# A gated unit and a long convolution on one core: the inverse transform's turn partly moved from DRAM to VectorE, and its neighbours made longer

## The chip, the cores and the metric

The kernel runs on one core of a Trainium2 chip. The metric is the device time of one execution in microseconds (us). Of the kernel before three executions were timed: the median is 236.9 us, the lowest 236.68, the highest 237.43. A change of about 0.3% (0.7 us) is what such a measurement can still tell from no change.

The core has five engines with instruction streams of their own: TensorE (PE; its weight loads are PEld in the profile), VectorE (DVE), ScalarE (ACT), GpSimd (POOL) and SyncE (SP). SP here does nothing but issue DMAs, and ACT issues a few. Each engine works its instructions off in program order; between engines there are only semaphores.

## The reference

The input `x` has 2048 rows of 640. It is layer-normalized to `xn`, and three things are added up: `x` itself, a convolution branch A and a gated branch B.

```python
x = A_q
xn = _layernorm(x, axis=-1)
return x + _A_ref(xn, A_k, A_v, A_shift_k, A_ssm_k, A_ssm_D) + _B_ref(xn, B_w_gate, B_w_up, B_w_down)
# B:  h = sigmoid(xn @ w_gate) * (xn @ w_up);  h @ w_down           (640 -> 1728 -> 640)
# A:  k_shift = four shifted copies of k times four taps, summed;  kv = k_shift * v
#     y = causal convolution of kv with ssm_k along the 2048 rows (by a real FFT of length 4096)
#     y = y + kv * ssm_D;   result xn * y
```

## The kernel before

Row `16*p + b` of the sequence lies on partition `p`, block `b` (16 blocks). Branch B runs in four passes `t` of 512 rows: for each of 13 slices of the hidden size a gate product and an up product (`product`, L293, five 512-column matmuls each), the sigmoid on ACT (`gate_ev`, L302), the product of the two on DVE (`up_ev`, L308), then a last half slice (`both_*`) and the down products (`down_mm` L334, `pair_mm` L341, `rest_mm` L351), whose sums DVE adds to `x` (L345, L356).

Branch A runs in five chunks `c` of 128 channels, woven between the products. A chunk goes through these steps:

- `kv_op` (chain `k`): the four shifted products and three sums on DVE (L384, L388, L390), and the product with `v` (L393). Each operation covers half of the blocks (128x1024), so there are 16 per chunk. `h_turn` (L370) transposes the filter by 32x32 blocks on DVE.
- `st1_mm`, `st1_ev`, `wr1`: the first transform stage on PE, copies out of PSUM into `t1` by ACT or DVE (L256, L259), and a write to DRAM (`d1`).
- `rd2`, `st2_mm`, `st2_ev`, `prod`: the turned data is read back, second stage in 32x32 matmuls (L443), copies into `xz`, and the complex product with the filter on DVE (L456 shuffle, L458 product).
- `inv1_mm`, `inv1_ev`: first inverse stage (PE L472), copies into `ao` by ACT or DVE.
- `wr2`, `rdb`: the turn of the inverse. `ao` is written to DRAM (`d2`, L488 in one piece or L492 in two) and read back with another assignment of partitions into `bi` (L502), two reads per chunk.
- `inv2_mm`, `inv2_q`, `inv2_x`: second inverse stage (PE L511, eight 128-column matmuls per group `m`, four groups per chunk), the product with `xn` on DVE (L516, 128x512) and the addition to `x` on DVE (L521, 128x512).

`store` (L359) writes finished pieces of `x` out, all on SP's queue but the very last, which ACT issues.

The order is written out by hand: every step is appended to a chain named by a letter, and the string `ORDER` names, letter by letter, which chain emits its next step. `F`, `I` and `J` mean that a copy out of PSUM (`B`, `A`, `C`) goes to DVE instead of ACT. `TURNS` reorders two chains, the loads `m` and the stores `o`. So each engine's program order, SP's queue of DMAs among them, is this string's order. PSUM has two pools: `psC` (two buffers, branch A's stages) and `psG` (four buffers, the products of branch B and of `inv2_mm`).

Of the kernel before, what the change touches and what calls it, by code (L numbers as in the profile page):

```python
# [37 lines left out]
def _tables():  # L38
# [11 lines left out]
    tb = s1.transpose(3, 2, 1, 0) / 2048.0  # L50
# [15 lines left out]
def kernel(  # L66
# [57 lines left out]
    kxs = [res.tile([P, NB + 3, P], BF16, name="kx%d" % i) for i in range(2)]  # L124
# [233 lines left out]
    def store(b0, b1, lo, hi):  # L358
        (nc.scalar if b1 == NB and hi == DM else sync).dma_start(outr[:, b0:b1, lo:hi], x[:, b0:b1, lo:hi])  # L359
# [12 lines left out]
    def kv_op(c, n):  # L372

        d = cin[c]
        half, n = divmod(n, 8)
        lo, hi = 8 * half, 8 * half + 8
        sc = d["sc"]
        kx = kxs[c % 2]
        def sb(m):
            return sc[:, m:m + 1, :].to_broadcast((P, 8, P))  # L380

        if n == 0:
            d["acc"] = cv.tile([P, 8, P], BF16, name="acc")
            nc.vector.tensor_tensor(d["acc"][:, :, :], kx[:, lo + 3:hi + 3, :], sb(0), ALU.mult)  # L384
        elif n in (1, 3, 5):
            m = (n + 1) // 2
            d["tmp"] = cv.tile([P, 8, P], BF16, name="tmp")
            nc.vector.tensor_tensor(d["tmp"][:, :, :], kx[:, lo + 3 - m:hi + 3 - m, :], sb(m), ALU.mult)  # L388
        elif n in (2, 4, 6):
            nc.vector.tensor_tensor(d["acc"][:, :, :], d["acc"][:, :, :], d["tmp"][:, :, :], ALU.add)  # L390
        else:
            kv = d["kvh"][:, 0, lo:hi, :]
            nc.vector.tensor_tensor(kv, d["acc"][:, :, :], kv, ALU.mult)  # L393
# [19 lines left out]
    def st1_ev(c, n, copy=act_copy):  # L413
        d = chunks[c]
        if n % 2 == 0:
            d[n // 2] = cv.tile([P, 8, 2, P], BF16, name="t1", bufs=2)
        o = 4 * (n % 2)
        copy(out=d[n // 2][:, o:o + 4, :, :].rearrange("p b s c -> p s b c"), in_=pss[n][:, :, :, :])

    def wr1(c, k):  # L420
        h, part = divmod(k, 2)
        d = chunks[c]
        sync.dma_start(d["d1"][:, h, 8 * part:8 * part + 8, :], d[k].rearrange("p b s c -> p b (s c)"))

    groups = {}
    xz = cv.tile([P, 3, 3, 8, P], BF16, name="xz")

    def rd2(s):

        c, s4 = divmod(s, 4)  # L430
# [5 lines left out]
    def st2_mm(s):  # L436

        d = groups[s]
        d["ps"] = ps = [psC.tile([P, 2, 2, 2, P], F32, name="ps2", tag="c") for _ in range(2)]
        for e in range(2):  # L440
            for g in range(4):
                for q in range(NQ):
                    nc.tensor.matmul(ps[q // 2][quad(g), q % 2, e, :, :], lhsT=FW[quad(q), 8 * (s % 4) + 2 * g + e, :],  # L443
# [17 lines left out]
    def inv1_mm(y):  # L461
# [3 lines left out]
        if y2 == 0:  # L465
            d["d2"] = dr.tile([32, P, P], BF16, name="d2", bufs=NC)
# [9 lines left out]
    def inv1_ev(y, n, copy=act_copy):  # L476
        d = chunks[y // 2]
        if n == 0:
            d["ao", y] = kxs[1][:, 0:NB, :] if y >= 7 and y % 2 else cv.tile([P, 16, P], BF16, name="ao")[:, :, :]
        dst = d["ao", y].rearrange("p (s g e) c -> p g s (e c)", s=2, g=4)  # L480
# [3 lines left out]
    def wr2(y):  # L484
        c, y2 = divmod(y, 2)
        d = chunks[c]
        if 2 * y % 3 < 2:
            sync.dma_start(d["d2"][16 * y2:16 * y2 + 16].rearrange("r p c -> p r c"), d["ao", y])  # L488
# [5 lines left out]
    def rdb(c, n):  # L494

        d = chunks[c]
        if c >= 3 and n == 1:
            bi = kxs[0][:, 0:NB, :].rearrange("p (h b) c -> p h b c", h=2)
        else:
            bi = cv.tile([P, 2, 8, P], BF16, name="bi")[:, :, :, :]  # L500
        src = d["d2"].rearrange("r (q h b) c -> (r q) h (b c)", q=NQ, h=2)
        sync.dma_start(bi.rearrange("p h b c -> p h (b c)"), src[:, :, 1024 * n:1024 * n + 1024])  # L502
        d["bi", n] = bi

    def inv2_mm(c, m):

        bi = chunks[c]["bi", m // 2]
        chunks[c]["pb", m] = ps = psG.tile([P, 4, P], F32, name="psb", tag="g")
        for i in range(4):
            for h in range(2):  # L510
                nc.tensor.matmul(ps[:, i, :], lhsT=TB[:, h, 4 * m + i, :], rhs=bi[:, h, 4 * (m % 2) + i, :],  # L511
                                 start=(h == 0), stop=(h == 1))

    def inv2_q(c, m):
        chunks[c]["yx", m] = yx = cv.tile([P, 4, P], BF16, name="yx")
        nc.vector.tensor_tensor(yx[:, :, :], chunks[c]["pb", m][:, :, :], xn[:, 4 * m:4 * m + 4, c * P:(c + 1) * P],  # L516
                                ALU.mult)

    def inv2_x(c, m):
        xs = x[:, 4 * m:4 * m + 4, c * P:(c + 1) * P]  # L520
        nc.vector.tensor_tensor(xs, xs, chunks[c]["yx", m][:, :, :], ALU.add)  # L521
# [120 lines left out]
    for c in range(NC):  # L642
# [15 lines left out]
        for y in (2 * c, 2 * c + 1):  # L658
# [3 lines left out]
            step("W", wr2, y)  # L662
        for n in range(2):
            step("R", rdb, c, n)
        for m in range(4):
            step("d", inv2_mm, c, m)
            step("q", inv2_q, c, m)
            step("q", inv2_x, c, m)
        for n in range(16):
# [28 lines left out]
    mmmmgggmssggmuLuLmsggsZgmugmgmLsuuggsmgggsmkLkgkkkumsmgkusmmgkPgmullmlgulHmgsusgmHmuggDgggmkksuskkaA  # L698
    kkkanggkkHaTAAegKuHeawmtkegkkekLgugaAuAgkkaADLgguaawAukmgsgAkggTuLksakkkkkggsguuwLPAkmkaAsthgggsKaaH
    HwVAAugukggaamwsskKKrukkkwkkAAklgggauADkksVggTbwlguBgakssglBkkkAuspprgbBgguBkasnkaKKwIggthTuaAkaugAI  # L700
    suggawspHuLLklkVkkAkkawApggakaLsgkkAKkgeemgAceLPuuggrgHuuCCbBrekkwgVFgkgppDlkkaAauKAggwhsulbgtgBBrwk
# [43 lines left out]
```

## Time and profile before

| | |
|---|---|
| median of the runs | 236.9 us |
| the profiled execution's own time | 238.36 us |
| its span, first to last instruction | 236.5 us |
| PE busy | 227.2 us, 96% |
| DVE busy | 202.1 us, 85% |
| ACT busy | 134.7 us, 57% |
| DMA, queue of SP | 55.42 MB, 89.3% of 16 engines' span |

The span is what the profile explains; some 1.9 us of the profiled execution's time lie around it. Durations in the profile are those of single instructions and overlap by some hundredths of a microsecond where one follows another at once. A matmul's duration is longer than the step from one matmul to the next, because matmuls are pipelined.

### The profile page before, as it was taken

How to read it: one execution, taken by the hardware profiler on the slowest of the kernel's cores; microseconds unless marked ns; L12 is line 12 of the kernel's file. 1: busy time of each engine (PE TensorE's matmuls, PEld its weight loads, DVE VectorE, ACT ScalarE, POOL GpSimd, SP SyncE). 2: the span in 40 equal slices, each digit the busy share in tenths (PEclk: the TensorE clock that was granted, in tenths of full speed). 3: DMA queues.
4: the chain of work that ended last, by engine and by line, in shares of the span. 5: the costliest groups of instructions: out<-in, count | busy, mean ns of one | idle time of the engine just before them, and what ended most of it. 6: DMA issues, size and time to landing. Idle time of an engine off the chain costs nothing.

```text
span 236.5 us, 5598 instructions
## 1 busy us (share of the span) xinstructions
PE 227.2 (96%) x2281; PEld 112.0 (47%) x2281; DVE 202.1 (85%) x321; ACT 134.7 (57%) x197; POOL 12.1 (5%) x27
## 2 busy tenths in 40 slices
PE   8999999979999999999999999999999999999990
PEld 2854444436444444447444445445654444445480
DVE  5542983899898989999998999999999999999591
ACT  2458521368886686993976566566365684651000
POOL 4210020000040000020000000000000000000000
PEclk9999999999999999999999999999999999999998
DMA  6999997997999997799999996899999885684775
GB/s 181 305 264 267 256 306 180 236 230 209 231 274 276 301 238 208 140 226 306 282 245 255 298 333 138 219 242 257 247 288 269 224 237 176 173 247 110 222 242 160
DMA packets 98223, 56.13 MB, mean 237 GB/s; under 512 B 56342, under 2 KB 92438, under 8 KB 98070
## 3 DMA queue, kind: packets, MB, share of 16 engines
q1 hardware_dynamic: 97622, 55.42, 89.3%
q8 instruction: 18, 0.29, 0.5%
q10 hardware_dynamic: 576, 0.36, 0.5%
q14 instruction: 7, 0.06, 0.1%
HBM read 35.45 MB, written 18.35 MB: 228 GB/s over the span
## 4 chain that ended last, share of the span: by engine, by line
PE 63%; DVE 15%; SPq 9%; DMA 8%; issue 3%; DVEq 0%
PE pg L293 16%; PE pu L293 16%; PE pd L334 13%; PE pr L351 4%; DMA kx<-in_A_k_dram 4%; PE ps L409 4%; PE ps L411 4%; DMA w<-in_B_w_up_dram 3%; DVE yx L516 3%; PE ps L443 2%; PE psa L472 2%; SPq L185 2%; DVE x L521 2%; SPq L188 2%; DVE xz L458 2%
## 5 line engine op out<-in xcount | busy, mean ns | idle before, releaser
L293 PEld LDWEIGHTS <-w 128*128 128x128 bf16 x500 | 47.0, 98 | 58.1 <-issue 4.8
L293 PE MATMUL pu<-xnT,w 128*128 128x512 bf16 x250 | 62.3, 380 | 0.0
L293 PE MATMUL pg<-xnT,w 128*128 128x512 bf16 x250 | 62.2, 379 | 0.0
L334 PE MATMUL pd<-wd,hT 128*128 128x512 bf16 x208 | 48.4, 379 | 0.3 <-DMA wd<-in_B_w_down_dram 0.2
L308 DVE TENSOR_TENSOR hT<-sig,pu 128x512 bf16<-128x512 bf16 x52 | 35.0, 682 | 12.5 <-PE pu L293 6.8
L302 ACT ACTIVATE sig<-pg 128x512 bf16<-128x512 f32 x52 | 30.9, 601 | 23.8 <-PE pg L293 20.3
L256 ACT CAST xz<-ps 128x1024 bf16<-128x1024 f32 x33 | 32.4, 1017 | 16.8 <-PE ps L443 16.8
L256 ACT CAST t<-ps 128x1024 bf16<-128x1024 f32 x33 | 32.5, 1011 | 16.6 <-PE ps L411 14.7
L334 PEld LDWEIGHTS <-hT 128*128 128x128 bf16 x208 | 19.7, 98 | 24.9 <-issue 2.7
L458 DVE TENSOR_TENSOR xz<-xz 128x2048 bf16<-128x2048 bf16 x20 | 24.4, 1220 | 0.3
L390 DVE TENSOR_TENSOR acc<-acc,tmp 128x1024 bf16<-128x1024 bf16 x30 | 20.7, 689 | 0.6
L388 DVE TENSOR_TENSOR tmp<-kx,sc 128x1024 bf16<-128x1024 bf16 x30 | 20.7, 689 | 0.5
L409 PE MATMUL ps<-kvh,S1t 128*128 128x512 bf16 x40 | 15.2, 379 | 1.2 <-DVE kvh L393 1.2
L411 PE MATMUL ps<-kvh,S1t 128*128 128x512 bf16 x40 | 15.5, 387 | 0.0
L456 DVE STREAM_SHUFFLE xz<-xz 128x512 f32<-128x512 f32 x20 | 14.5, 725 | 0.0
L516 DVE TENSOR_TENSOR yx<-psb,xn 128x512 bf16<-128x512 f32 x20 | 13.7, 685 | 0.7
L351 PE MATMUL pr<-wd,hT 128*128 128x128 bf16 x224 | 14.2, 219 | 0.0
L351 PEld LDWEIGHTS <-hT 128*128 128x128 bf16 x224 | 13.1, 98 | 2.0 <-issue 0.6
L256 ACT CAST ao<-psa 128x1024 bf16<-128x1024 f32 x11 | 10.8, 1013 | 4.0 <-PE psa L472 2.6
L345 DVE TENSOR_TENSOR x<-pd,x 128x512 bf16<-128x512 f32 x16 | 10.6, 683 | 2.9 <-PE pd L341 2.3
L511 PEld LDWEIGHTS <-TBt 128*128 128x128 bf16 x160 | 10.1, 98 | 3.6 <-issue 0.7
L370 DVE STREAM_TRANSPOSE kvh<-hn 128x512 f32<-128x512 f32 x10 | 10.9, 1096 | 0.0
(62 smaller groups left out, 189.3 us busy)
## 6 DMA issues: line engine op xcount, KB each, us to landing
d<-t SPq DMA_DIRECT2D x20, 512.0 KB, 5.2
t<-d SPq DMA_DIRECT2D x20, 512.0 KB, 5.3
bi<-d SPq DMA_DIRECT2D x8, 512.0 KB, 8.6
d<-ao SPq DMA_DIRECT2D x6, 512.0 KB, 5.3
kx<-in_A_k_dram SPq DMA_DIRECT2D x10, 256.0 KB, 5.2
kvh<-in_A_v_dram SPq DMA_DIRECT2D x10, 256.0 KB, 5.4
hn<-in_A_ssm_k_dram SPq DMA_DIRECT2D x20, 128.0 KB, 5.8
x<-in_A_q_dram SPq DMA_DIRECT2D x3, 640.0 KB, 5.4
```

What stands on the lines that cost most here:

```text
L256: nc.scalar.copy(out=out, in_=in_)
L293: nc.tensor.matmul(pg[:, :], lhsT=w[:, c, u * UP + fc * P:u * UP + (fc + 1) * P], rhs=xnT[:, :, c, :], start=(c == 0), stop=(c == NC - 1))
L302: nc.scalar.activation(sig[fc][:, :], pgs[0, fc][:, :], ACT.Sigmoid)
L308: nc.vector.tensor_tensor(hT[:, fc, :], sig[fc][:, :], pgs[1, fc][:, :], ALU.mult)
L334: nc.tensor.matmul(pds[bb][:, :], lhsT=hT[:, fc, bb * P:(bb + 1) * P], rhs=wd[:, fc, 0:4 * P], start=(fc == 0), stop=(bb > 1 and fc == NFC ...
L351: nc.tensor.matmul(pds[t, b0][:, bb, :], lhsT=hT[:, fc, bb * P:(bb + 1) * P], rhs=wd[:, fc, 4 * P:DM], start=(fc == 0), stop=(fc == NFC - 1))
L388: nc.vector.tensor_tensor(d["tmp"][:, :, :], kx[:, lo + 3 - m:hi + 3 - m, :], sb(m), ALU.mult)
L390: nc.vector.tensor_tensor(d["acc"][:, :, :], d["acc"][:, :, :], d["tmp"][:, :, :], ALU.add)
L409: nc.tensor.matmul(ps[:, 0, :, :], lhsT=S1[:, h, :], rhs=cin[c]["kvh"][:, 0, 4 * n4:4 * n4 + 4, :], start=True, stop=True)
L411: nc.tensor.matmul(ps[:, 1, :, :], lhsT=S1[:, h, :], rhs=hp[:, 2 * n4:2 * n4 + 2, :, :], start=True, stop=True)
L458: nc.vector.tensor_tensor(z[:, 1:3, :, :], z[:, 0:1, :, :].to_broadcast((P, 2, 8, P)), z[:, 1:3, :, :], ALU.mult)
L516: nc.vector.tensor_tensor(yx[:, :, :], chunks[c]["pb", m][:, :, :], xn[:, 4 * m:4 * m + 4, c * P:(c + 1) * P], ALU.mult)
```

## The change

- **The inverse turn.** For chunks 0 and 1 it still goes through DRAM, now written in one piece per half chunk and read back by four DMAs, each into 32 partitions (`rdb(c, q)`), in place into `ao`. For chunks 2, 3 and 4 there is no DMA: `inv_turn` transposes `ao` in place on DVE, four operations of 128x512 four-byte elements per chunk. `ao` is now one tile for a whole chunk, its own for chunks 0 to 2, the memory of `kx` for chunk 3 and that of `t1` for chunk 4. The table `TB` is permuted to suit, and `rows` swaps two groups of some chunks so that each half of `ao` is written in order.
- **Shift products.** For chunks 1 to 4 each operation covers all 16 blocks (128x2048), eight operations per chunk in place of 16. Chunk 0 keeps its 16.
- **Residual sums.** `inv2_x` adds two groups at once (128x1024), ten operations in place of 20.
- **Stores.** Three stores of the last 128 columns go through ACT's queue (before: one).
- **Order.** `ORDER` and `TURNS` are new throughout, so loads, copies and products stand elsewhere on every queue. DVE copies out of PSUM are 19 in place of 21 (ACT's two more).

```diff
-    tb = s1.transpose(3, 2, 1, 0) / 2048.0
+    tb = (s1.transpose(3, 2, 1, 0) / 2048.0).reshape(32, NQ, 2, NB, P).transpose(1, 0, 2, 3, 4).reshape(P, 2, NB, P)
...
-    kxs = [res.tile([P, NB + 3, P], BF16, name="kx%d" % i) for i in range(2)]
+    kx2 = res.tile([P, 2, NB + 3, P], BF16, name="kx2")
+    kxs = [kx2[:, i, :, :] for i in range(2)]
+    t1 = res.tile([P, 2, 8, 2, P], BF16, name="t1")
...
-        (nc.scalar if b1 == NB and hi == DM else sync).dma_start(outr[:, b0:b1, lo:hi], x[:, b0:b1, lo:hi])
+        (nc.scalar if b1 > 11 and hi == DM else sync).dma_start(outr[:, b0:b1, lo:hi], x[:, b0:b1, lo:hi])
...
+        nb = 8 if c == 0 else NB
         half, n = divmod(n, 8)
-        lo, hi = 8 * half, 8 * half + 8
+        lo, hi = nb * half, nb * half + nb
...
+    def rows(s):
+        c, s4 = divmod(s, 4)
+        return c, s4 ^ (2 * (s // 2) % 3 == 2)
...
     def wr2(y):
-        c, y2 = divmod(y, 2)
+        d = chunks[y // 2]
+        r = slice(16 * (y % 2), 16 * (y % 2) + 16)
+        sync.dma_start(d["d2"][r].rearrange("r p c -> p r c"), d["ao"][:, r, :])
+
+    def rdb(c, q):
         d = chunks[c]
-        if 2 * y % 3 < 2:
-            sync.dma_start(d["d2"][16 * y2:16 * y2 + 16].rearrange("r p c -> p r c"), d["ao", y])
-            return
-        for n in range(2):
-            lo = 16 * y2 + 8 - 8 * n
-            sync.dma_start(d["d2"][lo:lo + 8].rearrange("r p c -> p r c"), d["ao", y][:, 8 * n:8 * n + 8, :])
...
+        src = d["d2"].rearrange("r (q h b) c -> q r h (b c)", q=NQ, h=2)
+        sync.dma_start(d["ao"][32 * q:32 * q + 32, :, :].rearrange("p (h b) c -> p h (b c)", h=2), src[q])
+
+    def inv_turn(c, n):
+        a = chunks[c]["ao"].bitcast(F32).rearrange("p r c -> p c r")[:, 16 * n:16 * n + 16, :]
+        nc.vector.transpose(a, a)
...
-    def inv2_x(c, m):
-        xs = x[:, 4 * m:4 * m + 4, c * P:(c + 1) * P]
-        nc.vector.tensor_tensor(xs, xs, chunks[c]["yx", m][:, :, :], ALU.add)
+    def inv2_x(c, n):
+        xs = x[:, 8 * n:8 * n + 8, c * P:(c + 1) * P]
+        nc.vector.tensor_tensor(xs, xs, chunks[c]["yx"][:, :, :], ALU.add)
...
-            step("W", wr2, y)
-        for n in range(2):
-            step("R", rdb, c, n)
+            if c < 2:
+                step("W", wr2, y)
+        for n in range(4):
+            step("R", rdb if c < 2 else inv_turn, c, n)
```

More of the change, by code (lines that the diff above doesn't have):

```diff
@@ L414, in st1_ev @@
         d = chunks[c]
-        if n % 2 == 0:
-            d[n // 2] = cv.tile([P, 8, 2, P], BF16, name="t1", bufs=2)
         o = 4 * (n % 2)
-        copy(out=d[n // 2][:, o:o + 4, :, :].rearrange("p b s c -> p s b c"), in_=pss[n][:, :, :, :])
+        copy(out=t1[:, n // 2 % 2, o:o + 4, :, :].rearrange("p b s c -> p s b c"), in_=pss[n][:, :, :, :])
     def wr1(c, k):
@@ L436, in st2_mm @@
     def st2_mm(s):
+        s4 = rows(s)[1]
         d = groups[s]
@@ L442, in st2_mm @@
                 for q in range(NQ):
[L443 removed]
+                    nc.tensor.matmul(ps[q // 2][quad(g), q % 2, e, :, :], lhsT=FW[quad(q), 8 * s4 + 2 * g + e, :],
                                      rhs=d["t2"][quad(q), 2 * g + e, :], start=True, stop=True)
@@ L464, in inv1_mm @@
         d = chunks[c]
-        if y2 == 0:
+        if y2 == 0 and c < 2:
             d["d2"] = dr.tile([32, P, P], BF16, name="d2", bufs=NC)
@@ L667 @@
             step("q", inv2_q, c, m)
-            step("q", inv2_x, c, m)
-        for n in range(16):
+            if m % 2:
+                step("q", inv2_x, c, m // 2)
+        for n in range(8 if c else 16):
             step("k", kv_op, c, n)
```

70 lines of the change are left out of this document (33 added, 37 removed).

## The prediction

> **What bounds the kernel now.** I read the page's busy times first, then the busy times by stage, with stages cut where a pass ends on PE, then the waits of PE, and last the end of the timeline.
>
> ```profile
> span 236.5 us, 5598 instructions
> PE 227.2 (96%) x2281; PEld 112.0 (47%) x2281; DVE 202.1 (85%) x321; ACT 134.7 (57%) x197; POOL 12.1 (5%) x27
> ```
> ```profile
> 7.00:57.70 50.70, 49.30 (x340) 26.41 (x339) 34.72 (x58) 26.45 (x49) 4.33 (x7) 1.00 1.03 249
> 57.70:111.80 54.10, 54.10 (x413) 25.49 (x411) 50.33 (x77) 41.20 (x67) 4.17 (x6) 1.00 0.94 244
> 111.80:170.40 58.60, 58.60 (x692) 27.40 (x691) 56.31 (x85) 37.37 (x46) 0.42 (x1) 1.00 0.95 249
> 170.40:210.30 39.90, 39.68 (x617) 18.56 (x615) 39.35 (x63) 25.61 (x33) 0.00 (x0) 1.00 0.82 231
> 210.30:231.30 21.00, 19.70 (x209) 11.94 (x207) 17.21 (x29) 1.90 (x3) 0.00 (x0) 1.00 0.70 204
> 231.30:236.50 5.20, 0.00 (x0) 0.00 (x0) 0.00 (x0) 0.00 (x0) 0.00 (x0) 0.87 0.55 157
> ```
>
> The columns are the stage, its length, then PE, PEld, DVE, ACT, POOL busy (instructions), granted clock, DMA share and GB/s. PE is busy nearly everywhere, at full clock. Its matmuls are the same 2281 before and after, so there is little to win inside: PE's visible idle time from 7.0 to 231.3 is 50.70-49.30 + 39.90-39.68 + 21.00-19.70 = 2.9 us, of which about 0.9 lie behind its last matmul, so 2.0 us. DVE is the second bound: idle 3.8 us in pass 1, 2.3 in pass 2, 0.55 + 3.8 = 4.3 in pass 3 with its end. What the change does to DVE there decides.
>
> ```profile
> PE ps L409 <- DVE kvh L393: 1.2, 1, 1.2
> PE psa L472 <- DVE xz L456: 0.2, 1, 0.2
> PE psb L511 <- DVE yx L516: 0.2, 1, 0.2
> PE pd L334 <- DMA wd<-in_B_w_down_dram: 0.2, 1, 0.2
> PE pd L334 <- DVE yx L516: 0.2, 1, 0.2
> ```
>
> So PE's idle time is one wait of 1.2 us in pass 0 and four of 0.2. None is for the turn of the inverse: its DMAs are hidden, and taking them away gives PE nothing directly.
>
> **The change, part by part.** First DVE, since everything is paid there.
>
> ```profile
> L370 DVE STREAM_TRANSPOSE kvh<-hn 128x512 f32<-128x512 f32 x10 | 10.9, 1096 | 0.0
> L456 DVE STREAM_SHUFFLE xz<-xz 128x512 f32<-128x512 f32 x20 | 14.5, 725 | 0.0
> L458 DVE TENSOR_TENSOR xz<-xz 128x2048 bf16<-128x2048 bf16 x20 | 24.4, 1220 | 0.3
> L390 DVE TENSOR_TENSOR acc<-acc,tmp 128x1024 bf16<-128x1024 bf16 x30 | 20.7, 689 | 0.6
> L516 DVE TENSOR_TENSOR yx<-psb,xn 128x512 bf16<-128x512 f32 x20 | 13.7, 685 | 0.7
> L521 DVE TENSOR_TENSOR x<-x,yx 128x512 bf16<-128x512 bf16 x20 | 8.5, 423 | 0.4
> L259 DVE CAST xz<-ps 128x1024 bf16<-128x1024 f32 x7 | 8.5, 1219 | 0.2 <-PE ps L443 0.2
> L238 DVE TENSOR_SCALAR xn<-x,lnq 128x640 bf16<-128x640 bf16 x12 | 5.1, 442 | 0.2 <-POOL lnq L247 0.2
> ```
>
> Shift products: 64 operations of 0.689 become 32 of 128x2048, at 1.220 (the same shape and type as L458): -44.1 + 39.0 = -5.1 us. Residual sums: 20 of 0.423 become 10 of 0.689: -1.6. Copies: 21 become 19: -2.4. Transposes: 12 of 1.096: +13.2. Sum +4.1 us of DVE work. By pass, counted in the changed program's order (a pass ends with its addition of the rest product):
>
> - Pass 0: 22 shift operations become 16 and 6 long (+3.2), one more copy (+1.2): +4.4. DVE had 16.0 us idle there, so it is covered.
> - Pass 1: 42 become 18 long (-7.0), two more copies (+2.4), a normalization less (-0.4): -5.0. PE is full there (54.10 of 54.10), so this gains no time.
> - Pass 2: 16 become 8 long (-1.3), three more L516 (+2.1), one more shuffle (+0.7), 4 sums become 3 long (+0.4), a normalization more (+0.4): +2.3, against 2.3 idle.
> - Pass 3 with its end: all 12 transposes (+13.2), five copies fewer (-6.1), three L516 fewer (-2.1), 16 sums become 7 long (-1.9), one shuffle fewer (-0.7): +2.4, against 4.3 idle.
>
> Passes 2 and 3 together: 112.9 busy + 4.7 = 117.6 of 119.5 us. That fits with 1.9 us to spare, and durations overstate what DVE needs, since they overlap in a dense row of work. Three groups of eight L511 matmuls also move from pass 3 to pass 2. I take 0 for this part, with ends at -0.6 (the last three 0.2 waits gone) and +4 (next rival).
>
> The copies moved to ACT cost 2 x 1.0 us, hidden: ACT has 14 us idle from 170.4 to 210.3. Without that cover each would delay the group behind it by its own length.
>
> Pass 0's wait:
>
> ```profile
> 41.99 0.69 DVE L384 TENSOR_TENSOR acc<-kx,sc 128x1024 bf16<-128x1024 bf16 x1 [4.20 <-DMA kx<-in_A_k_dram]
> 48.55 0.39 PE L409 MATMUL ps<-kvh,S1t 128*128 128x512 bf16 x1 [1.22 <-DVE kvh L393]
> 36.48 4.49 SPq L151 DMA_DIRECT2D hn<-in_A_ssm_k_dram  x4
> hn<-in_A_ssm_k_dram SPq DMA_DIRECT2D x20, 128.0 KB, 5.8
> ```
>
> The late load was the second half of `k`. The change loads it earlier, and places 1.8 us more PE work ahead of the matmul. But DVE's new order puts the transpose of chunk 1's filter ahead of the last sum and product with `v`, and that filter now comes behind 0.29 MB more on SP's queue (second half of `v` and of chunk 1's `k`, taps; less chunk 1's first half and halo). Before, it landed by about 40.97 + 5.8 = 46.8; 0.29 MB at 249 GB/s is 1.2 us, so 48.0. Then 1.10 + 0.69 + 0.69 make 50.4, against 47.33 + 1.8 = 49.1 on PE: a wait of 1.3 in place of 1.2. What is late next is thus `hn`. I take 0, ends -1.2 and +1.5.
>
> ```profile
> 5.30 1.03 SPq L185 DMA_DIRECT2D w<-in_B_w_gate_dram  x1
> w<-in_B_w_gate_dram SPq DMA_DIRECT2D x5, 320.0 KB, 5.7
> 12.50 1.24 PE L293 MATMUL pg<-xnT,w 128*128 128x512 bf16 x5
> ```
>
> The weight loads are reordered too. The gate weights of slices 4 and 5 were issued at 5.30 and there by 11.0; four products of 1.08 from 12.50 on come first, so they are needed at 16.8. Three loads with 0.51 MB are put ahead of them, 2.1 us at 249 GB/s: 13.1, still hidden by 3.7. I cost it at 0; without that cover it would be the 2.1.
>
> DMA: three chunks lose 1 MB written and 1 MB read, 6 of 56.1 MB, and SP 11 issues. PE never waited for these, so 0. What is left:
>
> ```profile
> d<-ao SPq DMA_DIRECT2D x6, 512.0 KB, 5.3
> bi<-d SPq DMA_DIRECT2D x8, 512.0 KB, 8.6
> 57.73 1.08 PE pg L293 x5
> 189.43 0.44 PE L443 MATMUL ps<-t,FWt 32*32 32x256 bf16 x32
> L256 ACT CAST ao<-psa 128x1024 bf16<-128x1024 f32 x11 | 10.8, 1013 | 4.0 <-PE psa L472 2.6 <-issue 1.4
> 142.31 0.36 SPq L488 DMA_DIRECT2D d<-ao  x1
> 152.23 0.58 SPq L502 DMA_DIRECT2D bi<-d  x1
> ```
>
> Chunk 0's turn has less room: from its last L472 to its first L511 there were 15 products and some 4 us of other matmuls, about 20 us; now 15.5 (12 products of 1.08, four pairs of L409 and L411 of two matmuls like L293's, 0.43, two groups of L443, 0.4); chunk 1 has 14.5 by the same count. The way: two copies 2.0, write 0.4 + 5.3, four issues of 0.5, then the landing. With 5.3 (like a write of this size) that is 15.0 and hidden; with 8.6 it is 18.3, and PE waits 2.8. The reads now move runs of 8 KB into 32 partitions each, in place of 2 KB, so I take the short one, and 0.
>
> The end:
>
> ```profile
> 229.42 0.94 PE L351 MATMUL pr<-wd,hT 128*128 128x128 bf16 x14
> 230.81 0.43 DVE L521 TENSOR_TENSOR x<-x,yx 128x512 bf16<-128x512 bf16 x1
> 231.27 0.35 ACTq L359 DMA_DIRECT2D out_dram<-x  x1
> 231.58 1.62 SPq L359 DMA_DIRECT2D out_dram<-x  x3
> out_dram<-x SPq DMA_DIRECT2D x1, 96.0 KB, 2.6
> ```
>
> After the last addition (231.24) SP issues three more stores, the last from 232.74; it lands 2.6 later, 235.3, and 1.2 us close the span: 5.26 from the last addition to the end. Changed, the 128-column stores stand on ACT's queue, and SP has one left. So 0.35 + 2.6 + 1.2 = 4.15: -1.1 us. Ends -1.6 (the last addition is now the small one, some 0.4 after PE's end, not 0.88) and +0.5 (DVE comes late, the next case).
>
> Sum: 0 + 0 + 0 - 1.1, a span of 235.4 and 237.3 for the profiled execution in place of 238.36, which stands 1.5 above the median. On the median: 236.9 - 1.1 = 235.8 us.
>
> **A rule that speaks against it.** The shuffle reads and writes in order and takes 0.725 us; L370 moves as many elements, reads them 32 bytes apart, writes in order, and takes 1.096. So a strided side costs up to 0.37. The in-place transposes are strided by 256 bytes on both sides, which no row shows.
> The Trainium skill ("SBUF — State Buffer", Door 1: The DMA port swizzle) says that SBUF has 16-byte lines and that each access that crosses to a new line pays; by it the writes would pay as well as the reads. The rows agree for the read side.
>
> **The rivals.**
> - DVE becomes the bound of pass 3 (slower). Place: the transposes. If the second strided side costs as much as the first, each takes 1.47, and 12 x 0.37 = 4.4 us come on top. From 1.096 + 1.9/12 = 1.25 us each the spare 1.9 us are gone and DVE decides. Price 4.4 - 1.9 = 2.5, and with the stores 236.9 - 1.1 + 2.5 = 238.3. For it: L370 against L456. Against it: a read and a write side may overlap.
> - The turn through DRAM that is left holds PE (slower): 2.8 for chunk 0, 236.9 - 1.1 + 2.8 = 238.6; for both chunks about 3.8 more, 242.4. For it: the 8.6 above. Against it: 6 MB less on the queue.
> - The new order also closes PE's waits: -1.2 - 0.6 - 1.1, 234.0. For it: DVE's 5.0 us less in pass 1. Against it: `hn`.
>
> **How the numbers follow.** The forecast, PE stays the bound and the end is shorter (235.0 to 236.6): 0.42. All waits closed (233.2 to 235.0): 0.13. DVE bound: 0.27. DRAM turn or a load holds PE: 0.18. Range 233.2 to 240.8: it leaves out the double DRAM wait and transposes much above 1.47. Faster by over 0.3%, below 236.2: 0.29 + 0.13 = 0.42; within: 0.11 of the forecast and 0.04 of the two slow cases, 0.15; slower: 0.02 of the forecast and 0.41 of the slow cases, 0.43.
>
> **What would show it.** The mean of the transposes at about 1.1 us or well above 1.25; DVE's idle time from 111.8 to its end near 2 us; a wait of L409 in pass 0 for the product with `v`, behind `hn`; no wait of L511 for `ao`; the span ending 4.2 us after the last addition. Wrong it would be with PE waiting in pass 3 for PSUM that DVE has not cleared.

## The result, and the profile after

The changed kernel takes 239.1 us (median of 6 runs, 238.65 to 239.37) against 237.3 us for the kernel before on the same chip: ratio 1.0073, 95% interval 1.0048 to 1.0098. It is about 1.8 us slower; the forecast was 1.1 us faster. The profiled execution has its own time of 239.31 us at a span of 237.5, against 238.36 and 236.5 before.

The busy times of the changed kernel, then its busy times by stage, cut where passes 0, 1 and 2 end on PE, at 212.90 in pass 3, and at the end of the last addition. The columns are those of the rows shown before the prediction.

```profile
span 237.5 us, 5528 instructions
PE 226.6 (95%) x2270; PEld 111.6 (47%) x2281; DVE 207.0 (87%) x289; ACT 136.6 (58%) x199; POOL 11.7 (5%) x27
```
```profile
7.00:55.48 48.48, 48.26 (x335) 26.05 (x335) 34.23 (x54) 23.68 (x44) 4.34 (x7) 1.00 1.08 259
55.48:109.98 54.50, 54.29 (x413) 25.63 (x413) 51.89 (x62) 41.74 (x68) 3.71 (x6) 1.00 0.96 248
109.98:173.27 63.29, 61.27 (x753) 29.43 (x755) 58.62 (x80) 37.67 (x46) 0.42 (x1) 1.00 0.99 244
173.27:212.90 39.63, 39.06 (x576) 17.79 (x573) 38.49 (x57) 27.86 (x36) 0.00 (x0) 1.00 0.36 108
212.90:233.20 20.30, 18.20 (x197) 10.64 (x184) 19.53 (x27) 3.44 (x5) 0.00 (x0) 1.00 0.28 91
233.20:237.50 4.30, 0.00 (x0) 0.00 (x0) 0.00 (x0) 0.00 (x0) 0.00 (x0) 0.96 0.62 188
```

PE's work is the same 2281 weight loads (some matmul records are missing from the trace), but where they stand has shifted. Stage by stage, these two executions differ so:

- Pass 0 is 2.2 us shorter (48.48 against 50.70). PE's records in it fall by 1.0 (48.26 against 49.30), so about 1.2 of it is idle time gone.
- Pass 1 is level (54.50 against 54.10).
- Pass 2 is 4.7 us longer (63.29 against 58.60). 2.7 of that is PE work that stood in other passes before, in pass 3 most of all (61.27 against 58.60). The other 2.0 is idle time of PE, 1.7 of it in the first wait below, where it had waited for nothing at all.
- Pass 3 up to the last addition is 59.93 against 60.90, although PE has 2.1 us less to do in it (57.26 against 59.38). So 1.1 us of new idle time stand against the work that left.
- The end, from the last addition to the end of the span, is 1.0 us shorter (4.30 against 5.26), as forecast.

The waits of PE in the changed kernel (in all, how often, the longest):

```profile
PE pu L295 <- DVE hT L310: 1.7, 3, 1.2
PE psa L478 <- DVE xz L464: 0.9, 1, 0.9
PE psb L517 <- DVE hT L310: 0.6, 2, 0.3
```

Every new wait of 0.5 us or more in all is for VectorE. The first is in pass 2, the other two are in pass 3. Next the in-place transposes, and two other rows of VectorE:

```profile
L372 DVE STREAM_TRANSPOSE kvh<-hn 128x512 f32<-128x512 f32 x10 | 10.9, 1098 | 2.8 <-DMA hn<-in_A_ssm_k_dram 2.8
L386 DVE TENSOR_TENSOR acc<-kx,sc 128x2048 bf16<-128x2048 bf16 x4 | 4.9, 1220 | 1.5 <-ACT ao L258 1.4
L509 DVE STREAM_TRANSPOSE ao<-ao 128x512 f32<-128x512 f32 x4 | 4.6, 1207 | 0.0
L509 DVE STREAM_TRANSPOSE kx<-kx 128x512 f32<-128x512 f32 x4 | 4.6, 1208 | 0.0
L509 DVE STREAM_TRANSPOSE t<-t 128x512 f32<-128x512 f32 x4 | 4.4, 1194 | 0.1
```

An in-place transpose takes 1.20 us, between the forecast's 1.096 and the 1.25 from which VectorE was to decide. Last, the place in pass 2 where PE waits longest, in the timeline: VectorE, one DMA issue, and PE.

```profile
119.70 1.11 DVE L372 STREAM_TRANSPOSE kvh<-hn 128x512 f32<-128x512 f32 x1
122.19 1.23 DVE L386 TENSOR_TENSOR acc<-kx,sc 128x2048 bf16<-128x2048 bf16 x1 [1.38 <-ACT ao L258]
128.41 1.22 DVE L392 TENSOR_TENSOR acc<-acc,tmp 128x2048 bf16<-128x2048 bf16 x1
129.66 1.23 DVE L390 TENSOR_TENSOR tmp<-kx,sc 128x2048 bf16<-128x2048 bf16 x1
130.81 1.09 DVE L372 STREAM_TRANSPOSE kvh<-hn 128x512 f32<-128x512 f32 x1
131.82 1.24 DVE L310 TENSOR_TENSOR hT<-sig,pu 128x512 bf16<-128x512 bf16 x2
...
115.25 0.45 SPq L169 DMA_DIRECT2D kx<-in_A_k_dram  x1
...
132.51 1.24 PE L295 MATMUL pu<-xnT,w 128*128 128x512 bf16 x5 [1.21 <-DVE hT L310]
```

VectorE stands idle for 1.38 us ahead of the first shift product of chunk 4 (L386). That operation now covers all 16 blocks, so it needs both halves of `k`, and the second half was issued only at 115.25. The releaser that the row names is a copy into `ao`, which this product doesn't read. The load took 6.9 us to land, until 122.15, and the product starts right behind it. Then three operations of 1.1 to 1.2 us stand ahead of the gating product (L310) that PE needs to have a PSUM buffer back.

### The profile page after: what moved, and what is told of

It reads as the page before. It is cut to its first block, busy times and chain, and to the rows that moved or that the text cites. A ratio compares the mean times of both kernels' runs of the same rounds, so it can differ in the third digit from the quotient of the medians.

```text
span 237.5 us, 5528 instructions
## 1 busy us (share of the span) xinstructions
PE 226.6 (95%) x2270; PEld 111.6 (47%) x2281; DVE 207.0 (87%) x289; ACT 136.6 (58%) x199; POOL 11.7 (5%) x27
## 4 chain that ended last, share of the span: by engine, by line
PE 73%; DVE 18%; issue 3%; DMA 2%; SPq 1%; DVEq 0%; ACT 0%; ACTq 0%
PE pu L295 21%; PE pg L295 20%; PE pd L336 11%; PE pr L353 5%; PE ps L413 3%; PE ps L411 3%; DVE xz L464 2%; PE ps L449 2%; PE psb L517 2%; DVE hT L310 2%; PE psa L478 2%; DMA w<-in_B_w_up_dram 2%; DVE yx L524 2%; DVE t L509 2%; DVE xz L462 2%
## 5 line engine op out<-in xcount | busy, mean ns | idle before, releaser
L295 PEld LDWEIGHTS <-w 128*128 128x128 bf16 x500 | 47.1, 98 | 60.7 <-issue 7.0
L295 PE MATMUL pu<-xnT,w 128*128 128x512 bf16 x250 | 62.2, 379 | 1.7 <-DVE hT L310 1.7
L295 PE MATMUL pg<-xnT,w 128*128 128x512 bf16 x250 | 62.2, 379 | 0.0
L336 PE MATMUL pd<-wd,hT 128*128 128x512 bf16 x197 | 46.8, 379 | 0.8 <-issue 0.3
L310 DVE TENSOR_TENSOR hT<-sig,pu 128x512 bf16<-128x512 bf16 x52 | 34.4, 678 | 12.7 <-PE pu L295 9.6
L258 ACT CAST t<-ps 128x1024 bf16<-128x1024 f32 x32 | 31.6, 1011 | 18.2 <-PE ps L413 17.4
L336 PEld LDWEIGHTS <-hT 128*128 128x128 bf16 x208 | 19.5, 98 | 24.8 <-issue 2.7
L464 DVE TENSOR_TENSOR xz<-xz 128x2048 bf16<-128x2048 bf16 x20 | 24.4, 1220 | 0.3
L392 DVE TENSOR_TENSOR acc<-acc,tmp 128x2048 bf16<-128x2048 bf16 (+1 forms) x18 | 18.8, 1042 | 0.2
L390 DVE TENSOR_TENSOR tmp<-kx,sc 128x2048 bf16<-128x2048 bf16 (+1 forms) x18 | 18.7, 1041 | 0.2
L524 DVE TENSOR_TENSOR yx<-psb,xn 128x512 bf16<-128x512 f32 x20 | 13.3, 683 | 0.3
L258 ACT CAST ao<-psa 128x1024 bf16<-128x1024 f32 x9 | 8.8, 1014 | 5.3 <-PE psa L478 5.1
```

The source lines that it names most:

```text
L258: nc.scalar.copy(out=out, in_=in_)
L295: nc.tensor.matmul(pg[:, :], lhsT=w[:, c, u * UP + fc * P:u * UP + (fc + 1) * P], rhs=xnT[:, :, c, :], start=(c == 0), stop=(c == NC - 1))
L310: nc.vector.tensor_tensor(hT[:, fc, :], sig[fc][:, :], pgs[1, fc][:, :], ALU.mult)
L336: nc.tensor.matmul(pds[bb][:, :], lhsT=hT[:, fc, bb * P:(bb + 1) * P], rhs=wd[:, fc, 0:4 * P], start=(fc == 0), stop=(bb > 1 and fc == NFC ...
L390: nc.vector.tensor_tensor(d["tmp"], kx[:, lo + 3 - m:hi + 3 - m, :], sb(m), ALU.mult)
L392: nc.vector.tensor_tensor(d["acc"], d["acc"], d["tmp"], ALU.add)
```

## The experiments

The theory after this reading: the price of the stride (1.20 us for a transpose) in pass 3, and in pass 2 an order that makes PE wait for VectorE. The rivals: the late load of `k` alone; the order of VectorE's work in the last stage; the store queue; the longer operations. "Before" is the kernel before on the same chip in each comparison.

**The late half of k (a_k_early).** In the order of steps, chunk 4's second half of `k` is moved right behind its first half.

```diff
-    ...kkkuuKeCggDrah...suggAuplATHtKkkcsC
+    ...kkkuuKKeCggDrah...suggAuplATHtkkcsC
```

> The changed kernel with one load moved: the second half of chunk 4's k is issued right behind its first half (near 102 us) and not at 115.25. Theory 'long shift operation waits for both halves of k': DVE's wait of 1.4 us ahead of L386 at 122 goes, the three waits of PE for L310 in pass 2 (1.7 us) go, and the time falls by 1.5 to 2.2 us, to a ratio of 0.998 to 1.001 to the kernel before. Rival 'DVE is simply too full in pass 2, whatever it waits for': the wait moves elsewhere, the time falls by less than 0.5 us, ratio 1.005 to 1.008.

Measured: 239.39 us, 1.0070 (1.0038 to 1.0101). The idle time ahead of L386 is gone, and pass 2 is 62.04 us in place of 63.29. But it is gone as well in a_turn_flat and a_stores_sp, where the load stands as in the changed kernel: there it was issued at 115.5 and 115.8, landed in 5.2 us, and the product started at 120.8 and 121.1 without idle time. So this wait differs from execution to execution with the landing of the load. The time is not better: of the wait of L295 0.8 us stay, as in those two runs (0.9), and in pass 0 VectorE started on chunk 1's filter 1.6 us later (46.43 against 44.78). By the ratio its rival came true, and this late load is not what the change lost most by.

**The price of the stride (a_turn_flat).** The transposes go over adjacent elements of the same buffer; the kernel thereby leaves out the right turn of chunks 2 to 4.

```diff
-        a = chunks[c]["ao"].bitcast(F32).rearrange("p r c -> p c r")[:, 16 * n:16 * n + 16, :]
+        a = chunks[c]["ao"].bitcast(F32).rearrange("p r c -> p (r c)")[:, 512 * n:512 * n + 512].rearrange("p (c r) -> p c r", r=32)
```

> The changed kernel with the 12 in-place transposes over elements that lie next to each other, in place of 256 bytes apart on both sides. It leaves out the right turn: the blocks transposed are others than the result needs. Theory 'the stride on both sides is what makes a transpose 1.205 us': they take 0.72 to 0.75 us like the shuffle, DVE has 5.5 us less in pass 3, PE's waits of 1.5 us there go, and the time falls by 1.5 to 2.5 us, ratio 0.997 to 1.001. Rival 'the transpose itself is slow': they stay at 1.1 or above and the time falls by less than 0.5 us. Second rival, 'pass 3 is not bound by DVE's work': they are short and the time still falls by less than 0.5 us.

Measured: 237.06 us, 0.9993 (0.9964 to 1.0022). Its transposes:

```profile
L509 DVE STREAM_TRANSPOSE ao<-ao 128x512 f32<-128x512 f32 x4 | 2.6, 697 | 0.0
L509 DVE STREAM_TRANSPOSE kx<-kx 128x512 f32<-128x512 f32 x4 | 2.6, 688 | 0.0
L509 DVE STREAM_TRANSPOSE t<-t 128x512 f32<-128x512 f32 x4 | 2.5, 676 | 0.0
```

So the strides cost 0.51 us of 1.20 in each. Over twelve that is 6.2 us by the durations and 5.3 of VectorE's busy time (207.0 against 201.7), and 2.0 us of the kernel's time: more than the whole loss. A third or a little more of what VectorE is spared reaches the end. Of the 3.0 us between the two profiled spans 1.9 lie in pass 3 with its end (62.4 us in place of 64.2), where the transposes are; most of the rest is the wait in pass 2 that a_turn_flat's execution didn't have.

**Which side costs (a_turn_mix, one execution).** Chunk 2 reads strided and writes adjacent elements, chunk 3 the other way about, chunk 4 is as it was.

```diff
-        nc.vector.transpose(a, a)
+        b = chunks[c]["ao"].bitcast(F32).rearrange("p r c -> p (r c)")[:, 512 * n:512 * n + 512].rearrange("p (c r) -> p c r", r=32)
+        if c == 2:
+            nc.vector.transpose(b, a)
+        elif c == 3:
+            nc.vector.transpose(a, b)
+        else:
+            nc.vector.transpose(a, a)
```

> The price of each strided side, in one look: chunk 2's transposes read 256 bytes apart and write in order, chunk 3's read in order and write 256 bytes apart, chunk 4's do both as in the change. The turn of chunks 2 and 3 is left out by it, their blocks land elsewhere. Theory 'the read side pays': chunk 2 near 1.10 to 1.20, chunk 3 near 0.70. Rival 'the write side pays': the reverse. Rival 'each pays a part': both near 0.95.

```profile
L515 DVE STREAM_TRANSPOSE t<-t 128x512 f32<-128x512 f32 x4 | 4.4, 1195 | 0.1
L513 DVE STREAM_TRANSPOSE kx<-kx 128x512 f32<-128x512 f32 x4 | 4.3, 1066 | 0.1
L511 DVE STREAM_TRANSPOSE ao<-ao 128x512 f32<-128x512 f32 x4 | 4.3, 1065 | 0.1
```

One strided side costs 0.38 us, whichever it is; the second adds 0.13. The time of the single execution was 237.71.

**The order at the end (a_p_first).** On VectorE two gating products go ahead of three transposes of chunk 3, and the products with the spectrum (L464) of the last two groups ahead of other work, since PE waits 0.9 us for one of them. The diff shows the letters of the order there.

```diff
-    ...GRRRbuspgBggpBRpususcCCguqddgqqqodbqsBBgpodugsgppqcJ...
+    ...GRuRRbspgBggpuBRpsuscCCgupqddgqqqodbsBBgodugsgppqqcJ...
```

> The changed kernel with DVE's order alone changed in the last 30 us: two gate products ahead of three transposes of chunk 3, and the complex products of the last two groups ahead of three operations on chunks 2 and 3 that nothing waits for. The work is the same. Theory 'order of DVE's queue': PE's waits ahead of L517 (0.3) and L478 (0.85) shrink, the last L478 starts 1 us or more earlier than 218.7, the time falls by 0.8 to 1.5 us, ratio 1.001 to 1.004. Rival 'amount of work on DVE': what is moved back is waited for instead, the time falls by less than 0.4 us.

Measured: 239.31 us, 1.0064 (1.0036 to 1.0092). That wait fell from 0.9 to 0.4 us, but in its place come one of 0.6 for L524 and one of 0.4 for a turn through DRAM. So this order gains nothing: what is moved back is waited for in its place. Other orders of the last stage were not tried.

**The stores (a_stores_sp, b_k_stores).** The rule of the stores is put back in the changed kernel; and it is put into the kernel before, together with the load of the next experiment.

```diff
-        (nc.scalar if b1 > 11 and hi == DM else sync).dma_start(outr[:, b0:b1, lo:hi], x[:, b0:b1, lo:hi])
+        (nc.scalar if b1 == NB and hi == DM else sync).dma_start(outr[:, b0:b1, lo:hi], x[:, b0:b1, lo:hi])
```

> The changed kernel with the store rule of the kernel before (only the very last store on ACT's queue). Prediction's step on the end: the time from the last addition to the end of the span grows from 4.3 us to about 5.3, the time rises by 0.8 to 1.2 us, ratio 1.010 to 1.013. Rival 'SP issues fast enough, the end is set by the last addition': no change within 0.3 us.

> The kernel before with the earlier load of chunk 0's second half of k and the changed store rule (three stores on ACT's queue). Prediction's step on the end: the time from the last addition to the end of the span falls from 5.3 us to about 4.2, the time by 1.1 us against the earlier load alone, ratio 0.992 to 0.994. Rival, after the changed kernel kept its short end with all stores on SP: the end follows from which stores are left at the last addition and not from their queue; ratio 0.996 to 0.999.

Measured: a_stores_sp 238.8 us, 1.0042 (1.0017 to 1.0068), which overlaps the changed kernel's interval; from its last addition (ending at 232.42) to the end of its span (236.6) it takes 4.2 us, no longer than with the new rule. b_k_stores takes 236.95, the same as b_k_early without the rule, and its end is 5.3 us as in the kernel before. So the queue of the stores is worth nothing that these runs can tell. The reason that is left, and that no run tests by itself, is that the last addition has become the small one: here is the end of the changed kernel, VectorE and both queues.

```profile
231.69 0.69 DVE L529 TENSOR_TENSOR x<-x,yx 128x1024 bf16<-128x1024 bf16 x1
232.30 0.68 DVE L347 TENSOR_TENSOR x<-pd,x 128x512 bf16<-128x512 f32 x1
232.91 0.28 DVE L358 TENSOR_TENSOR x<-pr,x 128x128 bf16<-128x128 f32 x1
...
232.42 1.81 ACTq L361 DMA_DIRECT2D out_dram<-x  x3
...
230.03 4.07 SPq L361 DMA_DIRECT2D out_dram<-x  x5
```

Before, the addition of 128 columns for four blocks (128x512) came last, and SP had three stores still to issue, until 233.20: 1.96 us behind the end of that addition. In the changed kernel its last issue ends at 234.10, 0.91 behind.

**The load that made the kernel before wait (b_k_early, repeated as b_k_again).** In the kernel before, chunk 0's second half of `k` is loaded ahead of the down weights.

```diff
-    TURNS = {"m": [..., 18, 12, 13, 14, 8, 22, 17, 11, 20, ...],
+    TURNS = {"m": [..., 18, 12, 13, 11, 14, 8, 17, 22, 20, ...],
```

> The kernel before with one edit: the second half of chunk 0's k is loaded ahead of the down weights (and chunk 1's halo behind them). Theory 'pass 0 was won by this load alone': DVE's wait of 4.2 us ahead of L384 and PE's wait of 1.2 us ahead of L409 go, pass 1 starts near 56.3 in place of 57.6, ratio 0.994 to 0.996. Rival of the prediction, 'the filter hn is late next': PE still waits 1 us or more in pass 0, ratio 0.998 to 1.001. Third, 'the down weights come too late': PE waits for wd by 1 us.

> The kernel before with chunk 0's second half of k loaded ahead of the down weights once more, for a comparison with its neighbour on one chip: 236.95 us before, the same within 0.4 us here. If it is 237.5 or more, its gain over the kernel before is not to be relied on.

Measured: 236.95 us, 0.9975 (0.9954 to 0.9996), and again 236.89, 0.9982 (0.9963 to 1.0002). The wait of L409 in pass 0 is gone from the trace. It is 1.2 us in the profiled execution of the kernel before, but the gain is only 0.2 to 0.6 us by the median of b_k_again and the two ratios. A likely reading is that the wait comes in some executions only, and that the one profiled was such a one: on the chip of b_k_again most executions of the kernel before lie between 236.74 and 239.02, those with the earlier load between 236.67 and 237.27. Of what the changed kernel seems to win in pass 0, no more than this is shown to count.

**The longer operations (a_split, b_long).** a_split does the shift products and sums of the changed kernel as two halves each, in the same places. b_long brings the long shift products of chunks 2 to 4 to b_k_early, with their second halves of `k` and `v` loaded earlier and an order of my own for them, without anything else of the change. (In the diff, a_split stands first, then b_long.)

```diff
-            nc.vector.tensor_tensor(d["acc"], d["acc"], d["tmp"], ALU.add)
+            nc.vector.tensor_tensor(d["accs"][:, part, :], d["accs"][:, part, :], d["tmps"][:, part, :], ALU.add)
...
-        lo, hi = 8 * half, 8 * half + 8
+        nb = 8 if c < 2 else NB
+        lo, hi = nb * half, nb * half + nb
```

> The changed kernel with each long shift operation of chunks 1 to 4 (128x2048) issued as two halves (128x1024) at the same place in the order. The prediction's step 'long operations save DVE 5.1 us': by it DVE gets 5.1 us more, and with DVE near its bound in passes 1 and 2 the time rises by 1 us or more, ratio 1.011 or above. Rival 'starts of short operations follow each other at 0.60 us, so two halves take 1.20 against 1.14 and the saving was only in the durations': within 0.5 us of the change, ratio 1.005 to 1.010.

> The kernel before with the earlier load of chunk 0's second half of k (236.95 us), and with the shift products of chunks 2 to 4 as eight operations of 16 blocks in place of sixteen of 8 (their second halves of k and v loaded earlier); turns and residual sums as before. DVE is spared 3 x (16 x 0.689 - 8 x 1.220) = 3.8 us by the durations. Theory 'PE bounds the kernel before, so longer operations of DVE alone are worth nothing': 236.5 to 237.4 us, DVE's busy time 3.8 us below that kernel's, PE's waits for DVE still under 0.6 us in all. Rival 'a long operation holds the gating products behind it up': a new wait of PE for L308 of some 0.8 us, 237.8. Rival 'DVE was a bound in places': 236.2 or less.

Measured: a_split 240.05 us, 1.0106 (1.0068 to 1.0144), some 0.8 us over the changed kernel. That lies between its two expectations, and the intervals overlap, so the time alone doesn't decide. Its busy VectorE does:

```profile
PE 226.8 (95%) x2270; PEld 111.6 (47%) x2281; DVE 208.9 (87%) x321; ACT 136.6 (57%) x199; POOL 11.4 (5%) x27
```

The halves cost 1.9 us more of VectorE (208.9 against 207.0), not the 5.1 that durations add up to, since operations overlap in a dense row: two products L310 of 0.68 us take 1.24 in the timeline above. b_long takes 250.39 us, 1.0544 (1.0506 to 1.0582). The wait of PE that stands out in it:

```profile
PE ps L410 <- DVE kvh L394: 7.8, 3, 3.6
```

PE stood three times before the first matmul of a chunk, since the last product of the long row now comes right ahead of it, where with halves the first half was done long before. These waits are 7.8 of the 13.4 us that it is slower than b_k_early; the rest was not taken apart. None of b_long's three expectations came true. VectorE's busy time fell by 2.7 us (202.0 in b_k_early, 199.3 here) where the durations say 3.8, but what long operations are worth in time the run doesn't say. It shows that they need an order around them.

**The turn back in DRAM, within the new order (a_dram3, a_dram4, a_pool3, a_pool4).** Chunk 2, or chunks 2 and 3, are turned through DRAM again. a_dram issues these writes and reads on SP's queue, a_pool on POOL's. The writes stand right behind the copies into `ao`; the reads stand at other places than the in-place steps had, and in a_dram three products of chunk 2 (`d`) are moved back for them. The diff shows the step in a_dram3, then the write in a_pool3.

```diff
-            step("R", rdb if c < 2 else inv_turn, c, n)
+            step("R", rdb if c < 3 else inv_turn, c, n)
...
-        sync.dma_start(d["d2"][r].rearrange("r p c -> p r c"), d["ao"][:, r, :])
+        (sync if y < 4 else nc.gpsimd).dma_start(d["d2"][r].rearrange("r p c -> p r c"), d["ao"][:, r, :])
```

> The changed kernel with chunk 2's turn taken back to DRAM (two writes, four reads), so that eight in-place transposes are left in place of 12. DVE has 4 x 1.205 = 4.8 us less in pass 3. Theory 'DVE's transposes at 1.205 us hold pass 3 up': pass 3 shrinks by 1 to 1.7 us as it did with the dense transposes, ratio 1.000 to 1.004. Rival 'the DRAM turn is late': L517 of chunk 2 waits for ao by 2 us or more, ratio 1.008 or above.

> The same for chunks 2 and 3: only the last chunk is turned on DVE, four transposes are left, 9.6 us less on DVE in pass 3. Theory: pass 3 comes to 57.5 us or less, as with the dense transposes, ratio 0.997 to 1.002. Rival 'after 4.8 us less DVE is no bound any more': the same as with chunk 2 alone, within 0.002. Rival 'the DRAM turn is late': a wait of L517 for chunk 3, ratio 1.005 or above.

> Chunk 2's turn through DRAM again, but its two writes and four reads stand on POOL's queue, which has nothing else to do in pass 3; SP's queue is left as in the change. Theory 'the 14 us of the version on SP's queue were reads of the second stage held up behind the write', and 'transposes at 1.205 us hold pass 3 up': no wait of L449 for t<-d, 4.8 us less on DVE, pass 3 at 58 us, ratio 1.000 to 1.004. Rival 'the DRAM turn is late wherever it is issued': L517 waits for ao by 2 us or more, ratio above 1.008.

> The same for chunks 2 and 3, four in-place transposes left. Theory: DVE 9.6 us less in pass 3, pass 3 at 57.5 us, ratio 0.996 to 1.001. Rival: L517 waits for the landing of chunk 3's turn by 2 us or more, ratio above 1.008.

Measured: 251.35 us (1.0585, 1.0538 to 1.0632), 251.08 (1.0571, 1.0533 to 1.0608), 247.87 (1.0439, 1.0401 to 1.0477) and 252.89 (1.0638, 1.0598 to 1.0678). All four are slower than every time that their theories allow. In a_dram3 the rival's wait for `ao` doesn't come, another does; in a_pool3 and a_pool4 the rival came true. The longest wait of PE in a_dram3, then the two queues: the issues of SP in a_dram3, and those of POOL and the wait of PE in a_pool3.

```profile
PE ps L449 <- DMA t<-d: 7.2, 2, 5.3
```
```profile
178.99 0.36 SPq L498 DMA_DIRECT2D d<-ao  x1
179.44 6.82 SPq L438 DMA_DIRECT2D t<-d  x3
186.38 3.18 SPq L504 DMA_DIRECT2D ao<-d  x4
```
```profile
179.36 1.17 POOL L498 DMA_DIRECT2D d<-ao  x1 [6.18 <-ACT sig L304]
186.96 1.99 POOL L504 DMA_DIRECT2D ao<-d  x4 [6.43 <-DMA d<-ao]
...
198.28 2.72 PE L517 MATMUL psb<-ao,TBt 128*128 128x128 bf16 x24 [6.79 <-DMA ao<-d]
```

On SP the write of 178.99 stands behind the copies into `ao`, and the reads L438 that PE needs first stand behind it. On POOL's queue that cause is taken away, and the way itself shows: written at 179.36, there by 186.9, read from 186.96, first used at 198.28, 19.5 us after the last copy. Here is the same way in the kernel before (last copy into `ao`, first read, first product of chunk 2), then the first product in the changed kernel.

```profile
178.51 1.22 DVE L259 CAST ao<-psa 128x1024 bf16<-128x1024 f32 x1
186.68 0.52 SPq L502 DMA_DIRECT2D bi<-d  x1
194.60 1.06 PE L511 MATMUL psb<-bi,TBt 128*128 128x128 bf16 x16
```
```profile
191.48 0.61 PE L517 MATMUL psb<-ao,TBt 128*128 128x128 bf16 x8
```

The kernel before used chunk 2 14.9 us after its last copy (179.73), the changed kernel 12.5 us after its own (178.96). So the way on POOL's queue was 4.6 us longer than it had been on SP's, and these four runs say nothing against the turn in DRAM as it stood before. The in-place turn shortened the way by 2.4 us, and the new order has used this up: with a way of 14.9 us PE would wait some 2 us in it, an estimate from these times.

**Single waits of the new order (a_u_first, a_u_flat, a_best).** a_u_first is a_k_early with the gating product that PE waits for (the first `u`) ahead of a filter transpose (`H`). a_u_flat adds the adjacent elements of a_turn_flat, and with them leaves out the right turn. a_best is a_u_first with two more moves of this kind: a gate product and an inverse product of PE ahead of chunk 0's, and one product with `xn` behind the last spectrum products of VectorE.

```diff
-    ...AgHgusuVpblg...
+    ...AguHgsuVpblg...
```

> The changed kernel with the earlier k load of chunk 4 (239.39 us), and in pass 2 one gating product (L310 of slice 5) moved on VectorE ahead of a filter transpose of 1.09 us; there PE waited 0.82 us for it. Theory 'pass 2 lost time because DVE's order puts long operations ahead of what PE needs': that wait is under 0.3, pass 2 is 61.4 us in place of 62.0, time 238.8. Rival 'DVE is full there, so the wait comes back at the next slice': a wait of 0.5 or more elsewhere in pass 2, pass 2 still 62, time 239.4.

> The same with in-place transposes over adjacent elements, which leaves the right turn out of chunks 2 to 4; it shows the rest of the new order without the price of the stride (237.06 us without the two moves). Theory 'pass 2 lost time by DVE's order': 236.4. Rival 'DVE is full there': 237.1. Should it come out below 236.6, the longer operations and the new order would have won what was forecast, but for the stride.

> The changed kernel with the two moves of the run before (238.06 us, where PE waited 1.5 us for chunk 0's turn and 0.9 us for a product of chunk 4), and two more: one gate product and the first inverse product of chunk 1 ahead of chunk 0's inverse products on PE, and one product with xn of 0.69 us put behind the last products with the spectrum on VectorE. Theory 'the new order still had about 2 us of waits of PE in it that are no part of the turn': both waits under 0.4, time 236.5 us, level with the kernel before or a little under it. Rival 'what is taken off one place of VectorE is missed at the next': the waits move, time 237.8 or more.

Measured: a_u_first 238.06 us, 1.0015 (0.9991 to 1.0040). PE's wait for L310 in pass 2 is gone, and the ratio is 0.0058 lower than the changed kernel's, 1.4 us (1.0 by the medians, which come from two chips). Against a_stores_sp, which has both delays of pass 2 in its order, it is 0.0027, which the intervals don't set apart; so the size of this step is known only roughly. Behind the wait another comes up, in the timeline of PE:

```profile
138.56 1.95 PE L517 MATMUL psb<-ao,TBt 128*128 128x128 bf16 x32 [1.55 <-DMA ao<-d]
```

That is chunk 0's turn through DRAM, the prediction's second rival. The profiled execution of a_u_flat, with the same order up to there, doesn't have it, so this wait, too, differs from execution to execution. a_u_flat takes 236.0 us, 0.9922 (0.9898 to 0.9946): without the price of the stride and without the two delays in pass 2, the new order is 1.8 us faster than the kernel before. a_best takes 240.52, 1.0137 (1.0100 to 1.0173): of the two waits that it was to close one is gone and one is 0.4 us, and new ones of 0.8, 0.5 and 0.5 us stand elsewhere, with pass 2 at 65.1 us from start to start (109.9 to 174.98). Its rival came true: the waits move. They make up only a part of the loss against a_u_first; the rest was not taken apart.

No run of the new order that makes the right turn beats the kernel before. The best version that computes the same is the kernel before with one load moved, 236.9 us.

## Why the prediction was wrong

- **DVE in passes 2 and 3, taken at 0: this step failed.** The amount of work was nearly right: 117.6 us busy was forecast for the two passes, and 58.62 + 38.49 + 19.53 = 116.6 is there, with transposes at 1.20 in place of 1.096. What failed is the conclusion that 1.9 us of spare time let VectorE take any price up to 1.25 us for a transpose. The spare time isn't where the work is: in pass 3 VectorE is 97% busy (58.02 of 59.93 us), and in pass 2 it stood idle 4.7 us and was late all the same. At 1.20 us the stride already costs the kernel 2.0 us (a_turn_flat against the changed kernel, and again a_u_flat against a_u_first, 2.1). The size of the price is the smaller part of the miss: twelve times the 0.11 above the forecast's 1.096 is 1.3 us of VectorE, and if a third of it reaches the end, 0.4 us (an estimate; no run has transposes of 1.096). The rival "DVE becomes the bound of pass 3" was right in place and kind; its 1.47 us for two strided sides was too much, its threshold too high. That its time of 238.3 is near the measured one is in part chance, since pass 2's delays aren't in it.
- **The rule that speaks against it.** One strided side costs 0.38 us, as the forecast took from two rows of the kernel before; the second, which no row showed, costs 0.13 more. The Trainium skill ("SBUF — State Buffer", Door 1: The DMA port swizzle) says that each access that crosses to a new 16-byte line pays, and sets no write apart from a read. By itself each side does pay alike here (1.065 and 1.066 against 0.69), so the runs agree; together they cost 0.51, not the 0.76 of a sum.
- **The savings of the shift products, -5.1 us.** Too large: a_split gives 1.9 us of busy time. In the row of passes 2 and 3 this mattered little, since few of them are there. In pass 1 VectorE's busy time was forecast to fall by 5.0 and rose by 1.6 (50.33 to 51.89), with no effect on the time, as forecast. Part of this is the cut, which the forecast made at VectorE's last addition and the rows make on PE: for passes 0 and 1 together it is -0.6 forecast and +1.1 measured. Over the whole kernel VectorE's busy time rose by 4.9 us (202.1 to 207.0), where +4.1 was forecast.
- **Pass 0's wait, taken at 0.** The forecast that `hn` is late next is right in kind: VectorE waits 2.8 us for it. But the filter was there at 44.78 and not at 48.0, the product with `v` ended at 47.29 and not at 50.4, and PE came to it at 48.69. So PE doesn't wait behind it, and the wait of 1.2 us is gone with nothing in its place. By b_k_early such a wait is worth 0.2 to 0.6 us of the median. The forecast's own profile had it at 1.2 us.
- **What was left out: pass 2.** No step asked which load or which operation comes late there. The long first product of chunk 4 can wait for the second half of `k`, and three long operations then stand ahead of a gating product. Both moved away together give 1.4 us by the ratios to the changed kernel (a_u_first), with the doubt named there. The delay of the load alone gave nothing measurable.
- **The turn through DRAM that is left, taken at 0: right in the changed kernel.** PE never waits for it there. The new reads land 6.0 us after their issue in the median (the row below, from the DMA issues of the changed kernel), between the 5.3 that was taken and 8.6. The margin is small: with pass 2 tightened, the profiled execution of a_u_first has a wait of 1.5 us for it, that of a_u_flat has none.

```profile
ao<-d SPq DMA_DIRECT2D x8, 256.0 KB, 6.0
```

- **The end, -1.1: right in size (4.30 against 5.26), wrong in its reason.** Two runs show that ACT's queue has no part in it. That it follows from which addition is last is argued and not tested by itself; the forecast had the small last addition only in its lower end, -1.6.

In sum, by the ratios to the kernel before on each chip: the two delays in pass 2 0.0058 (1.0073 to 1.0015), the stride 0.0093 (1.0015 to 0.9922), and the rest of the change -0.0078, thus +1.4, +2.2 and -1.9 us. These three add up to the result because they are steps of one path, and each has an interval of some 0.6 to 0.8 us to either side. That the stride's step is of this size is borne out by a_turn_flat, which takes it alone (0.0080, 1.9 us). What the last part is made of is known only in part: the end is 1.0 us of it; what pass 0 and the fewer transfers add was not taken apart.

## What to carry to other kernels

When a change puts work on the second-busiest engine, spare time summed over a stage doesn't cover it. Look for the places where the bounding engine needs a result next, and ask how long the operations are that stand in line ahead of it there. A longer operation was cheaper for its engine here, but it waits for the last of its inputs, gives its first result late and keeps others waiting for all of its length. And before a wait in one profiled execution is counted as a gain, see whether the median and the profiles of other runs have it: the wait ahead of L386 and that for chunk 0's turn came in some profiles of the same order and not in others.

## What the runs showed that was not expected

- The 32-bit transposes of VectorE over 128x512 elements: 0.69 us with both sides adjacent, 1.065 with either side strided by 256 bytes, 1.20 with both.
- A turn of one chunk through DRAM took 19.5 us from the last copy to the first use on POOL's queue in a_pool3 (write 7.6, read 11.3), against 14.9 on SP's queue in the kernel before, though a single read of the changed kernel lands in 6.0 us in the median. In a_dram3 one write that had to wait on SP's queue held back reads of another chunk, and PE waited 5.3 us for them.
- The same load of 256 KB, the second half of chunk 4's `k`, landed in 6.9 us in the changed kernel and in 5.2 in a_turn_flat and a_stores_sp.
- PE's granted clock fell where it had stood still: in the ten microseconds of a_pool3 around its long wait it was 0.72, and 0.94 in the next ten (the column after POOL's, in its busy times by stage).

```profile
190.00:200.00 10.00, 3.21 (x54) 2.21 (x39) 1.36 (x2) 2.38 (x3) 0.00 (x0) 0.72 0.83 165
200.00:210.00 10.00, 10.00 (x147) 4.83 (x145) 8.24 (x14) 6.37 (x8) 0.00 (x0) 0.94 0.21 60
```

The span of a_pool3 is 7.5 us longer than the changed kernel's, for a wait of 6.8; that the lower clock makes up the difference was not tested.
